# Attention and SoLU feed-forward on one core: earlier exp, mult and norm behind h, spreads of the last group after the next stage's loads, another bank for the last product, results stored by quarters

## The chip, the cores and the metric

The kernel runs on one core of a Trainium2 chip. The metric is the device time of one execution in microseconds (us). A core has a matmul engine (TensorE, PE; its weight loads are listed as PEld), a vector engine (VectorE, DVE), an engine for activation functions and copies (ScalarE, ACT), a general one (GpSimd, POOL), and a queue engine (SyncE, SP) from which most transfers are issued. Each engine works through its own list of instructions in order; an instruction that needs another engine's result waits for a semaphore, and everything behind it on its engine waits too. PE writes to banks of PSUM, from which DVE and ACT read.

## What is computed

Attention with normed queries and keys, then a feed-forward block whose activation is h times softmax(h), followed by a layer norm. All is float32, except the two weight matrices, which come as float64.

```python
q_n, k_n = rmsnorm(q, g_q), rmsnorm(k, g_k)       # (8, 12, 448, 64)
attn = softmax(scale * q_n @ k_n^T)
x = (attn @ v) laid out as (3584, 768)
h = x @ w_in                                      # (3584, 1024)
e = np.exp(h - h_max)
solu = h * (e / (sum(e) + 1e-09))
ln = (solu - mu) / np.sqrt(var + 1e-06) * g_ln    # over the 1024
out = ln @ w_out                                  # (3584, 768)
```

## The kernel before, in words

There are two programs in the kernel; the one that runs is `fast_path`. The other, `general_path`, stands behind a branch at the very end (L1666) that is not taken: every engine reads a flag and jumps over it.

`fast_path` has three stages, each paced by PE.

1. Attention, to about 331 us. It isn't touched.
2. The first product, h = x @ w_in, to 584 us, in 14 groups (`NG`) of 256 rows. Each group is two tiles of 128 rows: tile 2g and tile 2g+1. A group is computed by Winograd's form of a 2x2 block product, that is, with seven products in place of eight (`products`, L968). Each of P1 to P7 is one *unit* of three float32 matmuls, six instructions in the trace, 2.58 us.
3. The second product, ln @ w_out, in seven passes of 512 rows (`NS`), each with seven outer products (`outer_product`, L1177) which are again made of seven inner ones.

Units run in a list that `in_parts` writes out by hand. From the second group on the order of one group is P6, P5, P7, then P1 of the next group, P4, P2 of the next group, P3. P6 and P7 add to the bank (A) that P1 of the same group opened; P3 adds to the bank (B) of P5; P2 has bank C and P4 bank D. Between P1 and P6, and between P6 and P7, ACT copies the bank's content to SBUF (`part`, L989; the copies are called q1, u2 and u3), so P6 must not start before the copy q1 is made, nor P7 before the copy u2. The rest is added on DVE by `plus` (L998), which reads a bank and a copy and writes a half row of h, with its maximum.

When P4 is done, tile 2g+1 of h is complete (`done(1)`); when P3 is done, tile 2g is (`done(0)`). For each complete tile there follows a chain over four engines:

- `ff_max` (L1047, DVE): the negated maximum;
- `ff_exp` (L1053, ACT): exp of h, with its sum;
- `ff_mult` (L1057, DVE): h times the exp;
- `ff_moments` (L1065 to L1070 on DVE, then L1071 and L1073 on POOL): mean and variance, scale and shift;
- `ff_norm` (L1077, ACT): scale and shift applied;
- `ff_spread` (L1086, DVE, a transpose of 32x32 blocks into `ub`; then four transfers from SP, L1089, to `ud` in DRAM).

`later(x, f)` puts a step x units further back in the order: x = 1 means right behind the unit that is being written out, 2 behind the next one. The five numbers in `WAITS` are those of exp, mult, moments, norm and spread. The instructions stand on each engine in the order in which these calls come; nothing reorders them afterwards.

On the same queues lie, in groups 0 to 6, the conversions of w_out from float64 (`convert_w`): two passes on ACT (L535, L536), two joins on DVE (L541, L542), a product on ACT (L547), and its load from SP; and, later, sums of w_out's blocks on POOL (`combine_out`, L563), 44 in all. POOL also makes the four block sums of each next group's x (L962 to L966).

The third stage works on operands that are loaded back from `ud` (`load_u`, L1131). Six halves for the first pass are loaded during the second stage; six more loads (four of them of data that were loaded before, into other memory) stand at the start of the third stage, since they take memory that the first product's weights and x hold until then. `make` builds the operands: a12 (L1151), a22 (L1153), a11 (L1149) are copies on ACT, s1 to s4 are sums on DVE (s2 is L1157, s3 L1159, s4 L1161), and `inner_sums` (L1172 to L1175) runs on POOL. Its units are counted in *slots* of 0.65 us, four to a unit of `later`. In the third stage every inner product adds to banks A, B or C, and copies on ACT (L1206) or sums on DVE (L1208, L1226, L1238, L1246) empty them; inner P7 waits for the copy u2 of inner P6, inner P4 for the copy u3 of inner P7, as before. `store_y` (L1260) sends one quarter of a pass's result, 256 rows by 384 columns (384 KB), when its last piece is there.

In PSUM the first product's banks A and C come from a pool of three buffers with the tag "t", B and D from one of two with the tag "o"; the banks of the third stage lie where these were.

Of the kernel before, what the change touches and what calls it, by code (L numbers as in the profile page):

```python
# [366 lines left out]
def fast_path(  # L367
# [24 lines left out]
    nc = tc.nc  # L392
    B, H, S, D = q.shape
    DM, DFF = moe_w_in.shape
    P = 128
# [6 lines left out]
    HO = DM // 2  # L402
    NT = B * S // P
    NG = NT // 2
# [563 lines left out]
    def products(g, done):  # L968


        k = {}
        n = DFF // 2

        def mul(bank, a, i, begin=True):
            a11, a12, a21, a22 = gs[g, "A"]
            sm = gs[g, "s"]
            a = {"a11": a11, "a12": a12, "s3": a21, "a22": a22, "s1": sm[:, 0], "s2": sm[:, 1], "s4": sm[:, 2]}[a]
            if begin:
                tag = "t" if bank in "AC" else "o"
                k[bank] = ps_t.tile([P, 512], FP32, tag=tag, name=bank, bufs=3 if tag == "t" else 2)[:, 0:n]  # L980
            for c in range(HD):
                nc.tensor.matmul(  # L982
                    k[bank], a[:, c], w_in[i][:, c],
                    start=begin and c == 0, stop=c == HD - 1, skip_group_check=not begin,
                )

        def part(name, bank):
            k[name] = sums_in.tile([P, 512], FP32, tag="part", name=name, bufs=4)[:, 0:n]
            nc.scalar.copy(k[name], k[bank])  # L989

        def plus(row, col, bank, x):
            t = 2 * g + row
            d = mt.setdefault(t, {})
            out = half_of(t, col)
            top = small.tile([P, 1], FP32, tag="top", name="top")
            nc.vector.tensor_tensor_reduce(  # L998
                out, k[bank], k[x], 1.0, d.get("top", -3.4e38), OP.add, OP.max, top
            )  # L1000
            d["top"] = top

        def p1():
            mul("A", "a11", 0)
            part("q1", "A")

        def p2():
            mul("C", "a12", 1)
            plus(0, 0, "C", "q1")

        def p6():
            mul("A", "s2", 5, False)
            part("u2", "A")

        def p5():
            mul("B", "s1", 3)

        def p7():
            mul("A", "s3", 4, False)
            part("u3", "A")  # L1020
            plus(1, 1, "B", "u3")

        def p4():
            mul("D", "a22", 6)
            plus(1, 0, "D", "u3")
            done(1)

        def p3():
            mul("B", "s4", 2, False)
            plus(0, 1, "B", "u2")  # L1030
            done(0)

        return {1: p1, 2: p2, 3: p3, 4: p4, 5: p5, 6: p6, 7: p7}

    def half_of(t, i):
        d = mt.setdefault(t, {})
        if "h" not in d:
            d["h"] = big.tile([P, DFF], FP32, tag="h", name="h", bufs=3)
        return d["h"][:, i * DFF // 2 : (i + 1) * DFF // 2]
# [4 lines left out]
    def ff_max(t):  # L1044
        d = mt[t]
        d["nmax"] = small.tile([P, 1], FP32, tag="hmax", name="hmax")
        nc.vector.tensor_scalar(d["nmax"], d["top"], -1.0, None, OP.mult)  # L1047

    def ff_exp(t):
        d = mt[t]  # L1050
        d["u"] = big.tile([P, DFF], FP32, tag="u", name="u", bufs=3)
        d["s"] = small.tile([P, 1], FP32, tag="hsum", name="hsum")
        nc.scalar.activation(d["u"], d["h"], AF.Exp, bias=d["nmax"], accum_out=d["s"])  # L1053
# [40 lines left out]
    def in_parts():  # L1094
        def done(g, i):
            t = 2 * g + i
            ff_max(t)
            for x, f in zip(WAITS, (ff_exp, ff_mult, ff_moments, ff_norm, ff_spread)):
                later(x, lambda f=f: f(t))

        p = [products(g, lambda i, g=g: done(g, i)) for g in range(NG)]
        parts = [p[0][1], p[0][2]]
        for g in range(NG):
            turn = [p[g][6], p[g][5], p[g][7], p[g][4], p[g][3]]
            x = len(parts)
            if g + 1 < NG:
                turn[3:] = [p[g + 1][1], p[g][4], p[g + 1][2], p[g][3]]
            parts += turn
            if g + 1 < NG:
                follow(parts, x, lambda g=g: sizes(g + 1))  # L1110
                follow(parts, x + 1, lambda g=g: block_sums(g + 1, 0))
                follow(parts, x + 2, lambda g=g: block_sums(g + 1, 1))
            if g + 2 < NG:
                follow(parts, x + 4, lambda g=g: load_x(g + 2))
        return parts

    WAITS = (1, 2, 3, 5, 7)
    ORDER = ("P1", "P5", "P6", "P2", "P7", "P3", "P4")
    STEP = 7
    PLACES = (0, 4, 8, 10, 12, 16, 20)  # L1120
    NS = NT // 4
    KC = HF // 2
    N2 = HO // 2
    HALVES = {"P1": ("a11", 0), "P2": ("a12", 1), "P6": ("s2", 5), "P5": ("s1", 3), "P7": ("s3", 4), "P3": ("s4", 2), "P4": ("a22", 6)}
    last = {}
    us = {}
# [50 lines left out]
    def outer_product(n, name, q):  # L1177


        operand_name, area = HALVES[name]  # L1180
        k = {}

        def mul(bank, a, i, begin):
            x = us[n, operand_name]
            sm = us.get((n, operand_name, "sums"))
            a = {
                "a11": x[:, 0, 0:KC], "a12": x[:, 0, KC:], "a22": x[:, 1, KC:],
                "s1": sm and sm[:, 0], "s2": sm and sm[:, 1], "s3": sm and sm[:, 2], "s4": sm and sm[:, 3],
            }[a]
            if begin:  # L1190
                tag = f"{bank}{q % 2}" + (str(q // 2 % 2) if bank == "A" else "")
                k[bank] = last["ps"].tile([P, 512], FP32, tag=tag, name=bank)[:, 0:N2]
            for c in range(KC):
                nc.tensor.matmul(  # L1194
                    k[bank], a[:, c].rearrange("p a i -> p (a i)"), w_out[:, area, i, c],
                    start=begin and c == 0, stop=c == KC - 1, skip_group_check=not begin,
                )

        def quarter(x, t, i):
            return x[:, t, i * N2 : (i + 1) * N2]  # L1200

        def plus(out, bank, t, i):

            x = {"P6": "Q1", "P2": "Q1", "P7": "U2", "P4": "U3", "P3": "V"}.get(name)
            if x is None:
                nc.scalar.copy(out, k[bank])  # L1206
            else:
                nc.vector.tensor_tensor(out, k[bank], quarter(us[n, x], t, i), OP.add)  # L1208

        def temp(x):  # L1210
            k[x] = last["u"].tile([P, N2], FP32, tag=x, name=x, bufs=3)
            return k[x]

        def result(t, i):
            return quarter(us[n, name], t, i)

        def p1():
            mul("A", "a11", 0, True)
            plus(temp("q1"), "A", 0, 0)

        def p2():
            mul("C", "a12", 1, True)
            us[n, name] = out_tile(name)
            if name in ("P1", "P6", "P7"):
                us[n, {"P1": "Q1", "P6": "U2", "P7": "U3"}[name]] = us[n, name]
            nc.vector.tensor_tensor(result(0, 0), k["C"], k["q1"], OP.add)  # L1226

        def p6():
            mul("A", "s2", 5, False)
            plus(temp("u2"), "A", 0, 1)  # L1230

        def p5():
            mul("B", "s1", 3, True)

        def p7():
            mul("A", "s3", 4, False)
            plus(temp("u3"), "A", 1, 1)
            nc.vector.tensor_tensor(result(1, 1), k["B"], k["u3"], OP.add)  # L1238

        def p4():  # L1240
            mul("A", "a22", 6, False)
            plus(result(1, 0), "A", 1, 0)

        def p3():
            mul("B", "s4", 2, False)
            nc.vector.tensor_tensor(result(0, 1), k["B"], k["u2"], OP.add)  # L1246
            if name in ("P2", "P3", "P4"):
                store_y(n, us[n, name], *{"P2": (0, 0), "P3": (0, 1), "P4": (1, 0)}[name])

        return [p1, p2, p6, p5, p7, p4, p3]  # L1250

    def out_tile(name):
        tag = "huhuhubb"[len(turns) % 8]
        turns.append(tag)
        x = big.tile([P, DFF], FP32, tag=tag, name=name, bufs=2 if tag == "b" else 3)
        return x[:, 0 : 2 * HO].rearrange("p (t n) -> p t n", t=2)

    def store_y(n, x, k, i):
        r = (4 * n + 2 * k) * P
        nc.sync.dma_start(  # L1260
            out[r : r + 2 * P, i * HO : (i + 1) * HO].rearrange("(t p) n -> p t n", p=P), x
        )
# [9 lines left out]
    def follow(p, i, f):  # L1272
        g = p[i]

        def both():
            g()
            later(1, f)

        p[i] = both
# [7 lines left out]
    def later(units, f):  # L1287
        todo.append((now + 4 * units, f))
# [49 lines left out]
    with tc.manual_schedule():  # L1338
# [233 lines left out]
        for n in range(NS):  # L1572
            base = period * n
            for i, name in enumerate(ORDER):
# [4 lines left out]
                x = HALVES[name][0]  # L1579
# [118 lines left out]
```

## Time and profile before

| what | us |
|---|---|
| median of three runs | 827.21 (824.08, 829.25, 827.21) |
| the profiled execution | 824.41 |
| its span, from first to last instruction | 822.2 |
| first product on PE, from first to last unit | 331.7 to 584.4 |
| first instruction of the last stage on PE | 585.23 |
| last DVE result / last store issued | 816.05 / 816.43 |

The span is the time between the first and the last instruction of the profiled execution; 2.2 us of its time lie around it. The granted clock of PE is 1.00 in nearly all of the span (0.997 in the mean). The page's groups of instructions and the trace in order of time are what the steps below are read from; in a line of the trace in order of time the columns are the start, the length, the engine, the line of the source, the operation and its tiles with their shapes, and in brackets the idle time before it and who ended it. A line for a stretch lists for PE, PEld, DVE, ACT and POOL the busy time and the number of instructions, then the clock, the share of the transfer engines and the rate.

Some durations, minimum, median and maximum in us over the first product: mult L1057 1.18, 1.22, 1.65; join L541 0.52, 0.56, 1.29; exp L1053 1.15 and its read-out 0.19; norm L1077 1.24; copy L989 0.57; POOL's L1071 0.55, 0.93, 1.48 and L1073 0.26, 0.27, 1.36.

### The profile page before, as it was taken

What the parts mean: (1) busy time and instruction counts of PE and PEld (TensorE: products, weight loads), DVE (VectorE), ACT (ScalarE), POOL (GpSimd) and SP (SyncE); (2) the same over time, 40 slices, a digit from 0 to 9 for tenths busy, and PEclk for the clock granted to TensorE, in tenths of its full rate; (3) what the DMA queues carried; (4) which work ended last, traced back from release to release, by engine and by line L of the source; (5) the groups of instructions that cost most, each with busy time, mean ns of one, the idle gap of its engine ahead of it and who ended that gap; (6) DMA issues with size and microseconds to landing.
All of it is one profiled execution on the core that took longest, in us unless ns stands there. A gap on an engine that the chain in (4) does not pass through costs nothing.

```text
span 822.2 us, 14988 instructions
## 1 busy us (share of the span) xinstructions
PE 800.5 (97%) x5030; PEld 468.7 (57%) x5030; DVE 618.1 (75%) x1217; ACT 474.6 (58%) x785; POOL 468.7 (57%) x635
## 2 busy tenths in 40 slices
PE   8989999999999999999999999999799999999996
PEld 4333444433334443444444444444499999999996
DVE  6867888887788888377878766677886866866945
ACT  6667778776777767366667644444424464464420
POOL 1334545555555647333356467777387777877861
PEclk9999999999999999999999999999999999999999
DMA  7678777777777663335665335552448466376312
GB/s 132 142 134 200 145 183 177 176 153 171 154 176 180 126 156 117 89 102 125 189 169 150 91 98 133 136 140 70 140 142 269 130 207 231 128 241 200 128 59 82
DMA packets 271938, 122.74 MB, mean 149 GB/s; under 512 B 190444, under 2 KB 257004, under 8 KB 271852
## 3 DMA queue, kind: packets, MB, share of 16 engines
q1 hardware_dynamic: 256668, 111.79, 52.9%
q10 hardware_dynamic: 15184, 9.90, 4.5%
q8 instruction: 42, 0.69, 0.4%
q14 instruction: 44, 0.36, 0.1%
HBM read 84.94 MB, written 36.70 MB: 148 GB/s over the span
## 4 chain that ended last, share of the span: by engine, by line
PE 84%; SPq 2%; DVE 2%; issue 2%; POOL 1%; DMA 1%; ACT 1%; POOLq 0%; ACTq 0%; DVEq 0%
PE A L1194 15%; PE A L982 13%; PE o L865 10%; PE s L812 10%; PE B L982 8%; PE B L1194 8%; PE D L982 4%; PE C L982 4%; PE sm L884 4%; PE C L1194 4%; SPq L634 2%; PE s L825 2%; PE o L854 2%; POOL ss L674 1%; DMA ur<-ud 1%
## 5 line engine op out<-in xcount | busy, mean ns | idle before, releaser
L802 ACT ACTIVATE E<-s 128x896 f32<-128x896 f32 x168 | 139.0, 935 | 14.9 <-PE s L812 14.6
L812 PE MATMUL s<-qkT 64*64 64x448 f32 x1152 | 121.3, 548 | 1.5 <-ACT E L802 0.9
L865 PE MATMUL o<-E,v 128*64 128x448 f32 x576 | 113.5, 543 | 0.0
L674 POOL COPY ss<-part 32x56 f32<-32x56 f32 x88 | 42.1, 478 | 97.9 <-DVE part L664 95.2
L713 POOL TENSOR_TENSOR qkn<-qk,ny 128x896 f32<-128x896 f32 x46 | 77.1, 1697 | 28.2 <-DMA qk<-in_k_dram 12.0
L1071 POOL TENSOR_TENSOR he<-he,mhalf 128x1 f32<-128x1 f32 x28 | 28.1, 1005 | 106.7 <-DVE he L1070 106.2
L812 PEld LDWEIGHTS s<-qkT 64*64 64x64 f32 x1152 | 47.5, 163 | 61.1 <-ACT E L802 31.3
L865 PEld LDWEIGHTS o<-E,v 128*64 128x64 f32 x576 | 39.2, 137 | 72.7 <-issue 66.4
L1194 PE MATMUL B<-w_out,sums 128*128 128x192 f32 x392 | 80.5, 328 | 0.0
L1194 PE MATMUL A<-w_out,sums 128*128 128x192 f32 x392 | 80.0, 327 | 0.4 <-DVE u L1208 0.4
L982 PE MATMUL B<-w_in,xsum 128*128 128x512 f32 x168 | 76.7, 592 | 0.0
L982 PE MATMUL A<-w_in,xg 128*128 128x512 f32 x168 | 74.7, 593 | 0.0
L1053 ACT ACTIVATE u<-h,hmax 128x1024 f32<-128x1024 f32 x28 | 32.2, 1148 | 65.2 <-DVE hmax L1047 65.2
L1194 PEld LDWEIGHTS B<-w_out,sums 128*128 128x128 f32 x392 | 67.0, 191 | 0.1
L1194 PEld LDWEIGHTS A<-w_out,sums 128*128 128x128 f32 x392 | 66.2, 190 | 0.9 <-POOL sums L1175 0.6
L664 DVE TENSOR_REDUCE part<-sq 128x28 f32<-128x896 f32 x46 | 48.7, 1080 | 8.8 <-ACT sq L656 6.7
L982 PEld LDWEIGHTS B<-w_in,xsum 128*128 128x128 f32 x168 | 31.9, 190 | 40.2 <-issue 38.3
L982 PEld LDWEIGHTS A<-w_in,xg 128*128 128x128 f32 x168 | 31.8, 190 | 40.2 <-issue 39.1
L723 DVE STREAM_TRANSPOSE qkT<-qkn 128x896 f32<-128x896 f32 x46 | 48.9, 1093 | 6.6 <-POOL qkn L713 6.6
L839 DVE TENSOR_TENSOR es<-E 128x896 f32<-128x896 f32 x48 | 53.3, 1112 | 0.5 <-ACT E L802 0.5
L656 ACT ACTIVATE sq<-qk 128x896 f32<-128x896 f32 x46 | 43.6, 985 | 8.7 <-DMA qk<-in_k_dram 6.7
L1194 PE MATMUL A<-w_out,s 128*128 128x192 f32 x224 | 45.6, 326 | 0.0
(151 smaller groups left out, 1625.3 us busy)
## 6 DMA issues: line engine op xcount, KB each, us to landing
ur<-ud SPq DMA_DIRECT2D x60, 256.0 KB, 4.7
ud<-ub SPq DMA_DIRECT2D x112, 128.0 KB, 2.3
xd<-xo SPq DMA_DIRECT2D x24, 448.0 KB, 3.7
qk<-in_q_dram SPq DMA_DIRECT2D x184, 56.0 KB, 2.5
qk<-in_k_dram SPq DMA_DIRECT2D x184, 56.0 KB, 2.4
v<-in_v_dram SPq DMA_DIRECT2D x24, 384.0 KB, 4.4
out_dram<-P SPq DMA_DIRECT2D x21, 384.0 KB, 3.8
raw<-in_moe_w_in_dram SPq DMA_DIRECT2D x12, 512.0 KB, 5.2
```

The costliest lines, as they stand in the source:

```text
L656: nc.scalar.activation(d["sq"], d["qk"].rearrange("p s b d -> p (s b) d"), AF.Square)
L664: nc.vector.tensor_reduce(norms[m]["part"][:, i], st[n]["sq"], AX, OP.add)
L674: e.tensor_copy(ss[g * 32 : g * 32 + 32], part[o * 32 : o * 32 + 32])
L713: e.tensor_tensor(d["qkn"], d["qk"].rearrange("p s b d -> p (s b) d"), y.rearrange("p b -> p b ()").to_broadcast([P, 2 * NB, 32]), OP.mult,)
L723: nc.vector.transpose(d["qkT"].rearrange("p s t -> p (s t)"), d["qkn"].rearrange("p b d -> p (b d)"))
L802: nc.scalar.activation(d["E", kc], s[:, :, 0:S], AF.Exp)
L812: nc.tensor.matmul(s[c : c + D, h, 0:S], d["qkT"][hh, 1, keys], d["qkT"][hh, 0, :], start=True, stop=True,)
L839: nc.vector.tensor_tensor(d["es"], d["E", 0], d["E", 1], OP.add)
L865: nc.tensor.matmul(d["o"][h * D : (h + 1) * D, :], quads[n // 2]["v"][:, n % 2 * 2 + h, kc], d["E", kc][:, h], start=False, stop=(kc == NJ ...
L884: nc.tensor.matmul(sm[g : g + 32, :], ones[:, w], e[:, h, t * S // 2 : (t + 1) * S // 2], start=(x == 0), stop=(x == len(terms) - 1),)
L982: nc.tensor.matmul(k[bank], a[:, c], w_in[i][:, c], start=begin and c == 0, stop=c == HD - 1, skip_group_check=not begin,)
L1194: nc.tensor.matmul(k[bank], a[:, c].rearrange("p a i -> p (a i)"), w_out[:, area, i, c], start=begin and c == 0, stop=c == KC - 1, skip_gr ...
```

## The change

Five edits. (1) The exp of a tile is written out at once when the tile is complete, and mult, moments, norm and spread follow 1, 2, 3 and 5 units behind instead of 2, 3, 5 and 7. Since 1 means right behind the same unit, mult now stands directly behind the tile's last plus on DVE. (2) For the two tiles of the last group the distances are 1, 2, 4 and 8. (3) In the last group P5 and P3 use a bank of the pool "t" and not of "o". (4) In the last pass of the third stage the outer products P3 and P4 are stored in four pieces each, of 128 rows by 192 columns (96 KB), as each piece is made, and not in one transfer of 384 KB at the end: eight transfers in place of two. (5) `store_y` is called for the same three outer products as before in all other cases.

```diff
-                tag = "t" if bank in "AC" else "o"
+                tag = "t" if bank in "AC" or bank == "B" and g == NG - 1 else "o"
...
             ff_max(t)
-            for x, f in zip(WAITS, (ff_exp, ff_mult, ff_moments, ff_norm, ff_spread)):
+            ff_exp(t)
+            for x, f in zip(LAST_WAITS if g == NG - 1 else WAITS, (ff_mult, ff_moments, ff_norm, ff_spread)):
                 later(x, lambda f=f: f(t))
...
-    WAITS = (1, 2, 3, 5, 7)
+    WAITS = (1, 2, 3, 5)
+    LAST_WAITS = (1, 2, 4, 8)
...
+        block = {"P2": (0, 0), "P3": (0, 1), "P4": (1, 0)}.get(name)
+        by_quarter = n == NS - 1 and name in ("P3", "P4")
+
+        def stored(t, i):
+            if by_quarter:
+                store_quarter(n, us[n, name], *block, t, i)
...
             nc.vector.tensor_tensor(result(0, 0), k["C"], k["q1"], OP.add)
+            stored(0, 0)
...
             nc.vector.tensor_tensor(result(1, 1), k["B"], k["u3"], OP.add)
+            stored(1, 1)
...
             plus(result(1, 0), "A", 1, 0)
+            stored(1, 0)
...
             nc.vector.tensor_tensor(result(0, 1), k["B"], k["u2"], OP.add)
-            if name in ("P2", "P3", "P4"):
-                store_y(n, us[n, name], *{"P2": (0, 0), "P3": (0, 1), "P4": (1, 0)}[name])
+            stored(0, 1)
+            if block and not by_quarter:
+                store_y(n, us[n, name], *block)
...
+    def store_quarter(n, x, k, i, t, half):
+        r = (4 * n + 2 * k + t) * P
+        c = i * HO + half * N2
+        nc.sync.dma_start(out[r : r + P, c : c + N2], x[:, t, half * N2 : (half + 1) * N2])
```

In the order of instructions this moves the following. On ACT the exp of tile 2g is now followed by the norm of tile 2g+1 and then by the copy u2 of the next group; before, u2 came ahead of that norm. On DVE mult and moments of tile 2g+1 now both stand ahead of the plus that completes tile 2g; before, mult stood ahead of it and moments behind it. On SP the four transfers of tile 24 now stand ahead of the third stage's first six loads (before: only those of tile 25), and the last group's transfers behind two more loads of the second pass.

## The prediction

> **What bounds the kernel now.** I read the page first (engine shares, the chain), then TensorE's waits, then three stages, then one group of the first feed-forward product on each engine.
>
> ```profile
> PE 800.5 (97%) x5030; PEld 468.7 (57%) x5030; DVE 618.1 (75%) x1217; ACT 474.6 (58%) x785; POOL 468.7 (57%) x635
> PE 84%; SPq 2%; DVE 2%; issue 2%; POOL 1%; DMA 1%; ACT 1%; POOLq 0%; ACTq 0%; DVEq 0%
> ```
>
> TensorE (PE) is the bound. Its waits list only two that the change can touch:
>
> ```profile
> engine line waited for: us in total, times, longest us
> PE A L1194 <- ACT u L1206: 4.5, 1, 4.5
> PE A L1194 <- DVE top L998: 0.9, 1, 0.9
> ```
>
> The stages of x@w_in, of the transition, and of the end (busy us per engine):
>
> ```profile
> 331.70:584.40 252.70, 252.68 (x592) 111.53 (x588) 179.26 (x384) 137.16 (x224) 139.96 (x160) 1.00 0.46 121
> 584.40:600.00 15.60, 10.24 (x51) 9.95 (x52) 12.64 (x28) 7.68 (x15) 6.57 (x9) 0.89 0.85 254
> 816.40:822.20 5.80, 0.00 (x0) 0.00 (x0) 0.01 (x1) 0.00 (x0) 0.00 (x0) 0.90 0.35 120
> ```
>
> In the first, PE idles 0.02 of 252.70 us: a shorter chain behind h can gain nothing there, only lose. In the second it idles 5.4; the end is 5.8. So some 11 us at most can be had. Now DVE, ACT and PE around one boundary of groups, in time:
>
> ```profile
> 390.52 1.18 DVE L1057 TENSOR_TENSOR u<-h,u 128x1024 f32<-128x1024 f32 x1
> 391.62 0.55 DVE L541 SCALAR_TENSOR_TENSOR tmp<-raw,tmp 128x384 uint32<-128x384 uint32 x1
> 392.68 0.74 DVE L998 CUSTOM_DVE_ANT_0 h<-B,u,top 128x512 f32<-128x512 f32 x1
> 393.54 1.28 DVE L1065 BATCH_NORM_STATS2 bs<-u 128x6 f32<-128x512 f32 x2
> 395.50 1.22 DVE L1057 TENSOR_TENSOR u<-h,u 128x1024 f32<-128x1024 f32 x1
> ```
>
> ```profile
> 393.65 1.15 ACT L1053 ACTIVATE u<-h,hmax 128x1024 f32<-128x1024 f32 x1 [0.24 <-DVE hmax L1047]
> 394.80 0.56 ACT L989 COPY u<-A 128x512 f32<-128x512 f32 x1
> ```
>
> ```profile
> 391.00 2.74 PE L982 MATMUL A<-w_in,xsum 128*128 128x512 f32 x6
> 393.58 2.74 PE L982 MATMUL B<-w_in,xsum 128*128 128x512 f32 x6
> 396.15 4.03 PE L982 MATMUL A<-w_in,xg 128*128 128x512 f32 x9
> ```
>
> P6 fills bank A from 391.00, P5 bank B, and P7 at 396.15 adds to A again: it may start only when ACT has copied u2 out of A. That copy ended at 395.36, 0.8 us in time. It stands right behind one exp.
>
> **The chain in order.** In the changed kernel's instruction order, ACT has between that exp (tile 2g) and u2 now also the norm of tile 2g+1 (L1077), and DVE has mult and moments of tile 2g+1 ahead of the plus (L998) that this exp waits for. I walk one group, zero being when plus takes D (350.00 in the first group; P7 starts 10.27 later, at 360.27).
> - exp starts 0.99 after (350.99) and is read out 1.24 later: 2.23. mult now waits for it, nothing hides that; DVE's next comes 1.13 on (585.28 to 586.41): 3.38.
> - plus of C, 0.62 (388.74 to 389.36): 4.00. Moments, 1.96 (393.54 to 395.50): 5.96.
> - plus of B to exp 0.97 (392.68 to 393.65): 6.93. Then 1.15 to ACT's next (393.65 to 394.80): 8.08. The norm's scale is ready 3.99 after the moments began (573.28 to 577.27): 7.99, just in time.
> - norm, 1.15 to ACT's next (593.86 to 595.01): u2 at 9.23; 0.56 and 0.06 to its reader (595.81 to 595.87): 9.85. Slack 0.42.
>
> Conversions of w_out share these queues in groups 0 to 6. The order puts a pair of joins (L541, L542: 1.06, 391.62 to 392.68) between moments and plus, and a product (L547, 0.6) between norm and u2, twice (u2 of groups 3 and 6): 9.85 + 1.06 + 0.6 - 10.27 = 1.24 late; another pair and a spread stand ahead of plus D there, so DVE also begins late, by 0 to 0.8; I take 0.4, so 1.64 each. Twice (groups 1 and 4) the pair L535, L536 (1.09, 397.08 to 398.17) stands between norm and u2: 0.67 late, once plus the 0.6 us that L535 waited for its raw DMA. Sum: 2 x 1.64 + 0.67 + 1.27 = 5.2. The nine other groups keep 0.42; POOL's shift (L1073) took 0.26 to 1.36 us, so some lose a little: 0.1 each, 0.9. **In-stage +6.1.** Bounds: 0 if the fast rows hold everywhere, and 11.6 if the nine lose 0.4 each (3.6) and both groups with joins meet slow ones (1.25 and 1.29 instead of 0.56 each, as at 365.28: 1.4 more, 2.8). A gain is excluded by the 0.02 us.
>
> On the joins: L542 took 1.23 at 343.80 beside POOL's L963, and 0.56 at 351.60 with POOL idle. The Trainium skill, page "SBUF — State Buffer", section "Who interferes with whom", says that a DVE instruction with two SBUF inputs contends with a GpSimd instruction that reads SBUF; mult (1.22, once 1.65) only partly agrees. By that rule the sum is up to 2.8 higher; I keep the fast row, the median.
>
> **Transition.** The last plus now reads a bank that A of the last stage doesn't take: the 0.85 us wait at 585.23 goes. What is late next: DVE takes the spread of tile 24 at 582.81 (in place of tile 25's), mult of tile 27 at 584.14 (its exp, 582.88 + 1.24, ends then), plus of B at 585.27 (was 584.41); exp of tile 26 starts at 586.24 (was 585.46) and the q1 copy behind it holds the second A product: the 0.85 is given back. On SP tile 24's four ud stores stand where tile 25's stood (584.09 to 585.92), so the six loads start at 586.03 as before. Then ACT, before:
>
> ```profile
> 593.34 0.62 ACT L1151 COPY a<-ur 128x512 f32<-128x512 f32 x1 [4.89 <-DMA ur<-ud]
> 593.86 1.24 ACT L1077 ACTIVATE u<-u,shift,he 128x1024 f32<-128x1024 f32 x1
> 595.01 0.60 ACT L1151 COPY a<-ur 128x512 f32<-128x512 f32 x1
> 595.51 0.30 ACT L1206 COPY u<-A 128x192 f32<-128x192 f32 x1
> ```
>
> The u3 copy at 595.51 ends the 4.5 us wait. Now tile 26's norm stands between the halves of a12 (before: tile 27's, ready by then). Tile 26: moments of 27 at 586.13 (plus + 0.86), mult at 588.09 (+1.96), two s2 from 589.22 (+1.13), P1's plus at 590.42 (+1.20), moments at 590.69 (+0.27), norm at 594.68 (+3.99), second a12 at 595.83 (+1.15), u3 at 596.33 (+0.50), PE at 596.69 (+0.36), against 595.87: **+0.8**. Fewer stores beside the loads (512 KB go earlier) may land a12 sooner, but the norm is then last. Bounds: L1071 took 0.55 to 1.48 us and 1.46 is in my row: -0.1 up to +0.8; a shift of 1.36 makes it +1.9. The spreads of the last group, 8 units out, pass two loads of n=1 on SP; PE idles 0.06 of 205 us from 600 to 805, so nothing.
>
> **End.** The last store is issued at 816.43 now too. SP's branch (L1666) at 816.9 is followed by its next instruction at 820.2, DVE's from 817.0 to 820.5; ACT, branching at 806.1, went on at 808.7. The store's landing (3.8 us by the page's median, about 820.2) and the branch end together. Eight quarter issues (about 0.4 each) are spread over 10 us; four in the last 1.7 us just fit, the last two 0.65 apart. A quarter lands sooner (128 KB ud: 2.3), the branch not surely: gain 0 if it stays 3.4, 0.8 if it becomes ACT's 2.6. **-0.4.**
>
> Page "DMA: Bandwidth & Descriptors", section "Anatomy of one DMA — SWDGE (gpsimd) path", gives about 2.0 us fixed per DMA, most of it the write receipt, which speaks against splitting stores. By it the last quarter lands at about 818.5, an estimate, and the branch alone decides.
>
> **Sum.** The profiled run is 824.41 (span 822.2 and 2.2 around), 2.80 under the median of three, 827.21. 824.41 + 6.1 + 0.8 - 0.4 = 830.9; with 2.8, **833.7** (+0.8%).
>
> **Rivals.** (a) Slower than 1%: one mechanism, DVE at its slow rows beside POOL at the boundary; it decides once a group's lag passes 0.42 us. In-stage 11.6, transition +0.8, end -0.4: 839. For: POOL is busy 140 of 252.7 us; against: medians are the fast rows. (b) The copies stay in time, because DVE's and ACT's queues run ahead of my walk (u2 had 0.8 spare here): in-stage 0, transition -0.85 as the bank's wait is saved whole, end -0.8: 825.6. Against: mult's wait for its exp and the norm ahead of u2 are in the order. (c) The losses come but half as large (raw DMAs early, DVE not late): 2.6, +0.5, -0.4: 830.
>
> **Numbers.** Forecast with (c), 829 to 835.4: 0.54; (a), above 835.5: 0.30; (b), 822 to 829: 0.16, of which 0.03 under 819. About 1% (8.3 us) is what a measurement of this kernel can tell from no change: faster 0.03, same 0.67, slower 0.30. The range 825.5 to 839.0 takes in (b)'s and (a)'s points.
>
> **What would show it.** PE waits "A L982 <- ACT u L989" of 0.7 to 1.6 us in four groups, none elsewhere; the first A of the last stage without wait, but three waits after it (q1, u2, u3), the last ending 12.3 us after the stage began; a last store of 96 KB landing well before the branch returns. PE without a gap before 584 would make me wrong, and then (b) holds.

## The result, and the profile after

The changed kernel took 836.2 us (median of four runs, 834.3 to 836.4) where the kernel before took 825.6 in the runs beside it: ratio 1.0122, 95% interval 1.0073 to 1.0172. The profiled execution took 834.3, its span is 832.2. Against the profiled execution of before (span 822.2) the 10.0 us more are made up so, read from the starts of TensorE's products: attention +0.5, x@w_in from its first to its last product 252.1 to 263.4 (**+11.3**), from there to the last product of the last stage 231.9 to 230.3 (**-1.6**), the end -0.1.

TensorE's waits, from the list of who waited for whom of the changed kernel (us in total, times, longest; L1196 and L1208 are L1194 and L1206 of before):

```profile
PE A L982 <- ACT u L989: 5.1, 4, 3.1
...
PE A L982 <- issue: 2.8, 3, 1.7
...
PE A L1196 <- ACT u L1208: 2.5, 2, 2.2
...
PE A L1196 <- ACT q L1208: 1.3, 1, 1.3
```

The wait for the bank (DVE top L998) is gone, the single wait of 4.5 has become three, and the first line is new: P7 waits for the copy u2. Some of the waits for u2 stand under "issue". From the starts of the products the waits ahead of P7 are 0.82 (group 1), 1.88 (3), 1.29 (4), 3.29 (6), and 0.56, 0.60 and 0.62 (9, 10, 13). The stages by windows (length, busy us of PE, PEld, DVE, ACT, POOL, granted clock, DMA share, GB/s):

```profile
332.15:595.95 263.80, 255.88 (x592) 111.51 (x589) 187.39 (x386) 135.68 (x224) 130.80 (x160) 0.99 0.44 118
595.95:611.55 15.60, 11.79 (x60) 10.73 (x59) 11.64 (x29) 8.52 (x17) 9.20 (x12) 0.89 0.77 236
```

In the first row PE idles 7.9 us instead of 0.02, and is busy 3.2 us longer with the same products; 1.4 of that is a stretch of half clock, shown below, and most of the rest lies around the restarts behind the waits. The longest wait, group 6, in time (start, length, engine, line, operation):

```profile
439.93 1.24 ACT L1077 ACTIVATE u<-u,shift,he 128x1024 f32<-128x1024 f32 x1 [0.97 <-POOL shift L1073]
...
442.17 0.57 ACT L989 COPY u<-A 128x512 f32<-128x512 f32 x1
...
442.77 0.69 DVE L998 CUSTOM_DVE_ANT_0 h<-B,u 128x512 f32<-128x512 f32 x1 [2.57 <-ACT u L989]
...
443.38 0.87 DVE L541 SCALAR_TENSOR_TENSOR tmp<-raw,tmp 128x384 uint32<-128x384 uint32 x1
443.81 1.31 POOL L966 TENSOR_TENSOR xsum<-xg,xsum 128x384 f32<-128x384 f32 x1
444.29 1.24 DVE L542 SCALAR_TENSOR_TENSOR tmp<-raw,tmp 128x384 uint32<-128x384 uint32 x1
...
446.61 0.70 DVE L998 CUSTOM_DVE_ANT_0 h<-D,u,top 128x512 f32<-128x512 f32 x1
...
452.34 2.74 PE L982 MATMUL B<-w_in,xsum 128*128 128x512 f32 x6
...
455.87 1.23 ACT L1077 ACTIVATE u<-u,shift,he 128x1024 f32<-128x1024 f32 x1
...
457.00 0.60 ACT L547 ACTIVATE w_out<-tmp,gcol 128x384 f32<-128x384 f32 x1
457.50 0.56 ACT L989 COPY u<-A 128x512 f32<-128x512 f32 x1
...
458.21 1.19 PE L982 MATMUL A<-w_in,xg 128*128 128x512 f32 x1 [3.13 <-ACT u L989]
```

P5's six products start 0.43 apart from 452.34, so P7 was due at 454.92; it started at 458.21. Ahead of u2 stand the norm and the product L547, as walked. But already the plus of D, the walk's zero, started at 446.61, where 10.27 before 454.92 is 444.65: DVE was 1.96 late. Ahead of it stand two joins that took 0.87 and 1.24 beside POOL's L965 and L966, and ahead of these a plus of B that had waited 2.57 for the copy u3 (442.17); that copy stood on ACT behind a norm (439.93) which had waited 0.97 for its shift. And what came behind the wait:

```profile
454.20:457.60 3.40, 0.88 (x3) 0.05 (x1) 2.02 (x5) 2.88 (x5) 0.76 (x1) 1.00 0.63 188
457.60:461.00 3.40, 2.79 (x4) 1.27 (x5) 2.80 (x8) 3.34 (x8) 1.51 (x3) 0.50 0.00 0
```

TensorE sat idle 2.5 of the first 3.4 us, and in the next 3.4 its granted clock is 0.50: the three products behind P7's first started 0.56, 0.42 and 0.42 later than they should.

### The profile page after: what moved, and what is told of

Its sections match the earlier page's. It is cut to its first block, busy times and chain, and to the rows that moved or that the text cites. A ratio compares the mean times of both kernels' runs of the same rounds, so it can differ in the third digit from the quotient of the medians.

```text
span 832.2 us, 14975 instructions
## 1 busy us (share of the span) xinstructions
PE 804.5 (97%) x5030; PEld 468.6 (56%) x5030; DVE 623.5 (75%) x1217; ACT 472.7 (57%) x785; POOL 460.6 (55%) x635
## 4 chain that ended last, share of the span: by engine, by line
PE 70%; SPq 6%; DVE 5%; DMA 3%; issue 3%; ACT 3%; POOL 1%; ACTq 0%; DVEq 0%; POOLq 0%
PE A L1196 15%; PE A L982 12%; PE B L1196 7%; PE o L865 7%; PE s L812 7%; PE B L982 6%; SPq L634 5%; PE D L982 4%; PE C L1196 4%; PE C L982 3%; PE sm L884 3%; DMA v<-in_v_dram 2%; PE s L825 1%; PE o L854 1%; DVE h L998 1%
## 5 line engine op out<-in xcount | busy, mean ns | idle before, releaser
L1071 POOL TENSOR_TENSOR he<-he,mhalf 128x1 f32<-128x1 f32 x28 | 18.1, 648 | 124.5 <-DVE he L1070 124.5
L1196 PE MATMUL A<-w_out,sums 128*128 128x192 f32 x392 | 80.8, 329 | 3.9 <-ACT u L1208 2.2
L982 PE MATMUL A<-w_in,xg 128*128 128x512 f32 x168 | 76.6, 605 | 7.9 <-ACT u L989 5.1
L1196 PE MATMUL B<-w_out,sums 128*128 128x192 f32 x392 | 79.8, 326 | 0.0
L1196 PEld LDWEIGHTS A<-w_out,sums 128*128 128x128 f32 x392 | 66.7, 191 | 4.8 <-issue 4.0
L1196 PEld LDWEIGHTS B<-w_out,sums 128*128 128x128 f32 x392 | 66.2, 190 | 0.1
L1057 DVE TENSOR_TENSOR u<-h,u 128x1024 f32<-128x1024 f32 x28 | 40.5, 1446 | 27.9 <-ACT u L1053 27.5
L563 POOL TENSOR_TENSOR w_out<-w_out 128x384 f32<-128x384 f32 x44 | 48.7, 1111 | 1.0
```

The source lines that it names most:

```text
L563: nc.gpsimd.tensor_tensor(o, p, q, OP.subtract)
L982: nc.tensor.matmul(k[bank], a[:, c], w_in[i][:, c], start=begin and c == 0, stop=c == HD - 1, skip_group_check=not begin,)
L1196: nc.tensor.matmul(k[bank], a[:, c].rearrange("p a i -> p (a i)"), w_out[:, area, i, c], start=begin and c == 0, stop=c == KC - 1, skip_gr ...
```

## The experiments

All of them together; "in" is x@w_in from first to last product, "out" from there to the last product of the last stage, both in us of the profiled execution; the ratio is to the kernel before on the same chip.

| kernel | in | out | ratio | 95% interval |
|---|---|---|---|---|
| before | 252.1 | 231.9 | | |
| changed | 263.4 | 230.3 | 1.0122 | 1.0073 to 1.0172 |
| old_chain | 252.1 | 233.3 | 1.0007 | 0.9989 to 1.0025 |
| norm_later | 254.7 | 230.5 | 1.0019 | 1.0000 to 1.0038 |
| moments_later | 257.4 | 230.6 | 1.0065 | 1.0042 to 1.0088 |
| norm_spread_later | 261.8 | 231.6 | 1.0139 | 1.0102 to 1.0175 |
| moments_spread_later | 259.0 | 234.6 | 1.0067 | 1.0041 to 1.0093 |
| stores_later | 253.2 | 232.4 | 0.9987 | 0.9967 to 1.0008 |
| conv_shift | 265.8 | 232.2 | 1.0138 | 1.0090 to 1.0185 |
| bank_only | 252.1 | 232.9 | 0.9990 | 0.9976 to 1.0004 |
| keep_busy | 252.4 | 233.4 | 1.0013 | 0.9999 to 1.0027 |
| best | 252.6 | 228.4 | 0.9956 | 0.9934 to 0.9978 |
| best2 | 252.1 | 226.6 | 0.9938 | 0.9914 to 0.9962 |
| best3 | 252.4 | 226.9 | 0.9922 | 0.9899 to 0.9945 |

### Is the loss the chain's? (old_chain)

```diff
-            ff_exp(t)
+            if g == NG - 1:
+                ff_exp(t)
+            else:
+                later(1, lambda: ff_exp(t))
...
-    WAITS = (1, 2, 3, 5)
+    WAITS = (2, 3, 5, 7)
```

> The changed kernel with the old chain behind h (exp, mult, moments, norm, spread in the old order) for groups 0 to 12; the last group's order, the bank of the last product and the stores by quarters stay changed. Theory (the whole loss lies in the chain of groups 0 to 12, on ACT and DVE ahead of the copy u2): the in-stage falls from 263.4 back to 252.1 +-0.5 us, PE shows no wait A L982 <- ACT u L989, and the time is that of before or up to 2 us less (the transition was 1.6 us shorter in the changed kernel's profile): 823.5 to 826 where before is 825.6. Rival (part of the loss lies in the other three edits, or the clock's half-speed stretch comes whatever the chain): 828 or more, or a half-speed stretch inside the in-stage without a gap.

The in-stage is that of before to the hundredth (252.11), with no wait in it; the time is 826.7 against 826.0, ratio 1.0007. So the whole loss is the chain's, in groups 0 to 12, and the other three edits bring nothing that can be measured. The shorter transition did not come along: with group 12's spreads at 7 again a transpose (1.24 us at 588.48) stood ahead of the moments of tile 26 on DVE, its norm waited 2.28 for the shift, and the copy u3 came late (a wait of 3.0 us); and 3.4 us of half clock lay over full work behind it.

### The norm ahead of u2 (norm_later)

```diff
-    WAITS = (1, 2, 3, 5)
+    WAITS = (1, 2, 4, 5)
```

> The changed kernel with the norm of groups 0 to 12 one part later (waits 1, 2, 4, 5 instead of 1, 2, 3, 5): on ACT the norm of tile 2g+1 stands behind the copy u2, DVE's order is the changed one, mult and moments ahead of the plus of B. Theory A (the norm ahead of u2 is the largest term, 1.15 of each group's lag; what DVE adds is the rest): each wait for u2 shrinks by 1.15, so the groups with 0.82, 1.88, 1.29, 3.29 us keep 0, 0.7, 0.1 and 2.1, the three of 0.6 vanish, and no gap reaches 3 us, so the clock keeps full speed: in-stage 255.0 (+2.9), time 827 (825.5 to 829). Rival B (mult and moments on DVE ahead of the plus of B hold the copies; the norm only waits beside them): the waits keep at least two thirds of their size, in-stage 259 or more, time 831 or more.

The in-stage fell by 8.7 us to 254.65 (2.9 over before was expected, 2.5 came), the time to 828.1. Of the four waits 0, 0.36, 1.39 and 0.64 are left, the three small ones and the half clock are gone. Theory A holds: one number out of place on ACT made three quarters of the loss. Group 6 lost more than the 1.15 of its norm, 2.65 (0.64 where 2.1 was expected): the same number had put a norm ahead of the copy u3 as well, and with that norm behind the copy the plus of D of group 6 is 0.45 late and not 1.96. But group 4 did not shrink (1.29 before, 0.1 expected). ACT's rows and SP's queue there (SPq are DMA issues):

```profile
415.27 0.66 ACT L535 ACTIVATE tmp<-raw,seven 128x384 f32<-128x384 uint32 x1 [1.46 <-DMA raw<-in_moe_w_out_dram]
...
416.39 0.57 ACT L989 COPY u<-A 128x512 f32<-128x512 f32 x1
```

```profile
401.18 5.97 SPq L1089 DMA_DIRECT2D ud<-ub  x8
407.26 8.07 SPq L515 DMA_DIRECT2D raw<-in_moe_w_out_dram  x8
```

Behind the norm stood another late thing: L535 waits 1.46 us for its raw load of w_out, and u2 stands behind L535. SP issued the eight ud stores of two tiles first, and then took 8 us over eight raw loads, because they wait for landings of the x-loads (SP's waits there: 4.6 us for xg<-xd, in two parts). All DMAs of the program take turns on eight semaphores (in this trace 100 or 101 DMAs on each), each waiting for the one eight places before it: the raw load issued at 413.17 waited for an x-load that landed at 413.15. An order of SP that puts a raw load eight places behind a long x-load makes it wait.

### Which part of the spread? (norm_spread_later, stores_later)

```diff
-    WAITS = (1, 2, 4, 5)
+    WAITS = (1, 2, 4, 7)
```

> As the kernel with the later norm (waits 1, 2, 4, 5), and with the spread back at 7: the ud stores of groups 0 to 12 stand on SP where they stood in the kernel before. Theory (what is left of the wait in group 4, 1.39 us, is ACT's L535 waiting 1.46 us for its raw load of w_out, which SP issued late because the ud stores now stand ahead of it and the loads share semaphores with the long xg loads): L535's wait falls to the 0.61 us of before, the wait for u2 in group 4 falls to 0.5 or less, the other two stay (0.36, 0.64): in-stage 252.9 to 253.7, time 826 to 827 where before is 826.0. Rival (the raw load is late because its buffer comes free late, when the joins on DVE read it, whatever the stores do): group 4 keeps 1.0 or more, in-stage 254.3 or more.

A miss: L535 no longer waits, as the theory had it, but the in-stage is 261.8, group 4 has still 0.94, groups 3 and 6 rose to 1.76 and 2.54, groups 5 and 9 to 12, which had no wait in norm_later, lost 0.24 to 0.67 each, and the half clock is back. The spread is a transpose on DVE and four stores, and the transpose (1.24) had moved with them to a place ahead of the moments and of the plus of B. exp's longest wait for hmax went from 4.8 to 6.0. So only the stores were moved:

```diff
-    WAITS = (1, 2, 4, 5)
+    WAITS = (1, 2, 4, 5, 7)
...
-            for x, f in zip(..., (ff_mult, ff_moments, ff_norm, ff_spread)):
+            for x, f in zip(..., (ff_mult, ff_moments, ff_norm, ff_turn, ff_store)):
```

> As the kernel with the later norm (waits 1, 2, 4, 5; in-stage 254.65 us), and the spread of groups 0 to 12 split: its transpose stays at 5, where it was, its four ud stores go to 7. Nothing moves on DVE, PE or POOL; only SP's order changes. (In the kernel with the whole spread at 7 the transpose, 1.24 us, had moved ahead of the moments and the plus of B, and the in-stage became 261.8: that run could not tell the stores apart.) Theory (the 1.39 us left in group 4 is L535's raw load, issued late on SP behind the ud stores and behind the landing of an xg load): L535 waits 0.7 or less in place of 1.46, group 4's wait is 0.7 or less, the others stay as they were (0.36, 0.64): in-stage 252.9 to 254.0, time 0.5 to 1.5 us under that kernel's. Rival (the raw load comes late for its buffer or for the busy DMA engines): 1.1 or more stay in group 4, in-stage 254.3 or more.

Group 4's wait and L535's are gone entirely, 0.37 and 0.64 stay in groups 3 and 6, in-stage 253.19. SP's queue of that kernel at the same place:

```profile
402.84 1.72 SPq L515 DMA_DIRECT2D raw<-in_moe_w_out_dram  x4
404.66 6.81 SPq L1092 DMA_DIRECT2D ud<-ub  x4
411.58 1.77 SPq L515 DMA_DIRECT2D raw<-in_moe_w_out_dram  x4
```

Now the stores wait for the x-load and nobody waits for them. With the norm one part and the stores two parts later than in the change, and mult, moments and transposes as early, the time is that of before (0.9987): the shorter chain is then free, and brings nothing.

### DVE's share (moments_later, moments_spread_later)

```diff
-    WAITS = (1, 2, 3, 5)
+    WAITS = (1, 3, 4, 5)
```

> As the kernel with the later norm, and with the moments one part later too (waits 1, 3, 4, 5): DVE takes the plus of B ahead of the moments of tile 2g+1; only exp and mult stand earlier than in the kernel before. Theory (mult alone costs 1.15 of DVE ahead of the plus of B, u2 has some 4 us to spare): in-stage 252.1 to 252.7, time 823.5 to 825.5 (the shorter transition kept). Rival (any reordering that puts mult, which waits for exp, ahead of the plus of C makes DVE late beside the conversions of w_out): waits for u2 stay in the groups 3 and 6, in-stage 254 or more, time 827 or more.

A miss, with the in-stage and the time on the rival's side: 257.4, with 0.98, 2.64 and 1.13 us in groups 3, 4 and 6. With the moments later the norms wait for their shift (12 times, 18.4 us in all, between 340 and 480 us; no such wait in norm_later), and in group 4 L535 waited 2.68 us for its raw load, 1.2 more than in norm_later, as group 4's wait did. The next run put the spread back as well (waits 1, 3, 4, 7).

> As the kernel with the later moments (waits 1, 3, 4, 5), and with the spread back at 7. That kernel's in-stage was 257.4, with a wait of 2.64 us for u2 in group 4, behind an L535 that waited 2.68 us for its raw load. Theory (SP's order made that wait): group 4 falls to 0.6 or less and the 0.98 and 1.13 us in groups 3 and 6 to half or less, since their u2 stands behind the same late loads: in-stage 252.1 to 253.5, time 825.5 to 827. Rival (plus of B ahead of the moments makes the norm late, and the norm the copies behind it, whatever SP does): 1.5 us or more stay in group 4, in-stage 255 or more, time 828.5 or more.

In-stage 259.0, not 253: 1.61, 2.13 and 1.35 us are left, and half clock behind the second. L535 still waited 1.9 us for its load in group 4, so the stores' old place alone did not bring the load in time. The run moved the transpose too, as above, so neither theory is settled by it: of the 2.7 us that the later moments cost, 1.2 go with L535's load, and what made the rest stays open. The version with late moments and only the stores late was not tried.

### Do the conversions size the waits? (conv_shift)

```diff
-            follow(parts, 3 * (x - n_in) + 2, lambda x=x: convert_next(x))
+            follow(parts, 3 * (x - n_in) + 3, lambda x=x: convert_next(x))
```

(The combinations on POOL one part later with them.)

> The changed kernel with the conversion of w_out (and its combinations on POOL) one part later: in the instruction order the joins ahead of the plus of B and the product L547 ahead of u2 now fall in groups 1, 4 and 7, the pair L535, L536 in groups 2 and 5, and groups 3 and 6 are free of both. Theory (the size of a group's wait is what the conversions put in its queues): waits for u2 of 1.6 to 3.3 us in groups 1, 4 and 7, of 0.7 to 1.4 in 2 and 5, none over 0.7 in 3 and 6; in-stage 262 to 266; a half-speed stretch only behind a gap of 3 us or so. Rival (groups 3 and 6 are long for another reason, their x-loads or POOL's sums): 1.5 us or more stay in 3 and 6.

The waits moved as the order says: 1.43 (1.6 was the least expected), 2.07 and 3.30 us in groups 1, 4 and 7, 0.87 and 0.94 in 2 and 5, none in 3 and 0.26 in 6. Group 7 is the image of group 6: a norm that waited 0.96 ahead of the copy u3, joins of 0.87 and 1.23, a plus of D that is 1.97 late. Its clock, though, behaves otherwise, and not as expected:

```profile
415.80:419.20 3.40, 1.49 (x4) 0.46 (x3) 2.58 (x4) 3.40 (x6) 0.00 (x0) 1.00 0.41 125
419.20:422.60 3.40, 3.40 (x6) 1.31 (x5) 2.86 (x7) 3.31 (x7) 2.54 (x4) 0.50 0.17 39
473.80:477.20 3.40, 2.26 (x6) 0.71 (x4) 2.02 (x6) 1.49 (x3) 1.09 (x2) 1.00 0.07 19
477.20:480.60 3.40, 1.40 (x4) 0.71 (x5) 3.17 (x8) 3.37 (x6) 0.21 (x1) 1.00 0.02 5
```

The 2.07 us of group 4 brought half clock (second row), the 3.30 us of group 7 did not: they fell into two windows of 3.41 us (1.18 and 1.96 idle), the 2.07 into one (1.91 idle).

### The bank alone (bank_only)

```diff
-                tag = "t" if bank in "AC" else "o"
+                tag = "t" if bank in "AC" or bank == "B" and g == NG - 1 else "o"
```

> The kernel before with one edit: the last group's bank B comes from tag t. Theory (the 0.85 us wait for the bank goes and is given back at the copy u3 behind the loads, 4.5 us): last in-stage product to last out-stage product unchanged within 0.3 us, time equal to before within 0.3%. Rival 1 (the wait is saved whole): 0.85 us less, 0.1%. Rival 2 (the shift of 0.85 us moves the half-speed stretch of 3.4 us off full work, as in the changed kernel): 1.5 to 2.5 us less, 0.25%.

The 0.85 us for the bank went and came back as 0.88 at the copy q1; u3's wait stayed (4.7). 0.9990, within what can be told from no change: the theory holds for the waits. Out grew by 1.0 where 0.3 was the most expected, since the half clock lasted 6.8 us here instead of 3.4.

### Is it the idle time that halves the clock? (keep_busy)

```diff
+        def keep_busy():
+            x = last["ps"].tile([P, 512], FP32, tag="C0", name="busy")[:, 0:N2]
+            a = us[0, "a11"][:, 0, 0].rearrange("p a i -> p (a i)")
+            for i in range(24):
+                nc.tensor.matmul(x, a, w_out[:, 0, 0, 0], start=i == 0, stop=i == 23)
+
+        when(15, keep_busy)
```

> The kernel before with 24 products of 128x192 more, into a bank that nothing reads, placed on TensorE ahead of the fourth quarter of the last stage's first product, where it stood idle for 4.7 us (nothing is left out; 24 x 0.163 = 3.9 us of otherwise idle time). Theory (the 3.41 us of half clock that begin at 595.7 in the kernel before, over full work, are the answer to the idle time just ahead of them): the granted clock stays 1.0 there, the out-stage shortens by 1.67 us, the time by as much: 823 to 824 where before is 824.6, and no wait grows. Rival (the half clock comes whatever TensorE does at that place, or the added products delay the copy u3): the stretch of 0.5 is still there, time equal or up to 1 us more.

The stretch of half clock was gone (granted clock 1.00 throughout, 0.51 there before), so it does answer to the idle time. The time was not better: the rows count these products as 48, and they took 7.8 us, not 3.9, some 2.8 beyond the end of the copy u3, more than the 1.7 won.

### The transition without its waits (best, best2, best3)

On the kernel before, with its chain and stores:

```diff
+    LAST_WAITS = {
+        2 * NG - 3: (1, 2, 3, 5, 7, 9), 2 * NG - 1: (1, 3, 5, 7, 8, 8), 2 * NG - 2: (2, 4, 5, 7, 9, 9),
+    }
...
+            waits = LAST_WAITS.get(t, WAITS + WAITS[-1:])
-            for x, f in zip(WAITS, (ff_exp, ff_mult, ff_moments, ff_norm, ff_spread)):
+            for x, f in zip(waits, (ff_exp, ff_mult, ff_moments, ff_norm, ff_turn, ff_store)):
...
-        for h in range(2):
-            for t in (2, 3):
-                load_u(0, t, h)
-        for t in range(2):
-            load_u(0, t, 1)
+        for t, h in ((0, 1), (1, 1), (2, 0), (3, 0), (2, 1), (3, 1)):
+            load_u(0, t, h)
...
-        made(0, "s2", 0, 3)
-        made(0, "s3", 6, 8)
-        made(0, "a12", 10, 11)
-        made(0, "a22", 12, 14)
-        made(0, "s4", 17, 20)
+        made(0, "s2", 0, 2)
+        made(0, "a12", 13, 14)
+        made(0, "s3", 17, 19)
+        made(0, "a22", 21, 22)
+        made(0, "s4", 24, 26)
```

with the bank of bank_only, and the next quad's loads, a11 and s1 up to 7 slots later.

> The kernel before with its own chain behind h, the other bank for the last product, and the start of the last stage reordered: the stores of tile 25 go behind the six loads, a12's two loads come first, a12 is made after the copy u3, s3, a22, s4 and the next quad's loads later, exp of tile 26 behind the copy q1, the norms of the last group behind u3 (stores as before). Theory (the 4.7 us wait and the 0.85 for the bank are nothing but ACT's order and SP's): in-stage 252.1, no wait over 1 us in the first 20 us of the last stage, last in-stage product to last out-stage product 231.9 - 5.5 = 226.4, and with no such gap no half-speed stretch there either, 1.7 less: time 819 (817.5 to 821.5). Rival (the work put off makes operands late further on, in the second or third product of the last stage): waits of 3 us or more in all come back there, time 823 or more.

0.9956: 3.6 us faster, half of what was expected. The waits of the transition (in the kernel before for the bank and for u3, in the changed one for q1, u2 and u3) and the half clock are gone; 3.7 us of other waits came further on (0.36, 1.53, 0.65, 1.12), so half of the rival is true too. best2 moves tile 26's moments and norm to 6 and 8 (its spread stays at 9, unlike what is said below) and the next quad's sums some slots on:

> The kernel with the reordered start of the last stage (252.6 in-stage, 3.7 us of waits in the last stage's first 26 us, span 821.6), with moments, norm and spread of tile 26 another part later (so POOL takes a12's sums ahead of tile 26's pow, and DVE the plus of the second product ahead of its moments) and s1, s2, s3, s4 of the next quad 1 to 11 slots later. Theory (what was left there was this one queue of moments and next operands): the waits of 1.53, 0.65 and 1.12 fall to 1.2 in sum, last in-stage product to last out-stage product 226.5 (228.4 before), time 1.5 to 2.5 us under that kernel's, ratio to before 0.993 to 0.994. Rival (DVE has more work than time in these 25 us, whatever the order): the waits come back elsewhere, 2.5 us or more in sum, ratio 0.9955 or more.

Out 226.6, as expected, with 0.35, 1.53 and 0.29 us of waits left, 2.2 in sum where 1.2 was expected; 0.9938. Its first 15.6 us of the last stage, where before PE worked 10.2 and the changed kernel 11.8 us:

```profile
579.65:595.25 15.60, 14.04 (x83) 13.21 (x82) 14.76 (x33) 9.20 (x20) 10.80 (x15) 1.00 0.49 134
```

> The last kernel with one number changed: the moments of tile 26 another part later (slot 23 in place of 19), so that on DVE the plus of the second product's last quarter (L1257) no longer stands behind them. Theory (the 1.53 us that was left at that quarter's bank B is DVE's 1.96 us of moments ahead of its plus): that wait falls to 0.5 or less, first to last out-stage product 225.1 to 225.6 (226.2 before), time 1 us less, ratio to before 0.992 to 0.994. Rival (DVE is full there, and the moments push the next plus instead): 1 us or more comes back within the next 20 us, ratio 0.994 as before.

The wait of 1.53 went, one of 1.56 and one of 0.5 came some 4 us later, at another plus of DVE: the rival holds, the row above shows why (DVE 14.8 of 15.6 us). best2 and best3 (0.9938 and 0.9922) can't be told apart; both beat the kernel before and the changed one.

## Why the prediction was right, and where it was not

The time, 836.2, lies in the range, but outside the forecast's own band (829 to 835.4): it is 0.7 into that of rival (a), which had a chance of 0.30. Against the kernel before it is +10.6 us where +6.5 was forecast. In the profile the in-stage cost 5.2 more than its sum and the transition 2.4 less, and the kernel before has a median 1.6 under the 827.2 that the sum was added to; that 836.2 came so near to 833.7 is in part luck. By its steps:

- **The walk of one group** was right to 0.1 us: from the plus of D to P7 it gave 9.85 + 1.06 + 0.6 = 11.51 for the groups with joins; the rows show 11.55 in group 3 and 11.60 in group 6. The groups it named were groups that waited. Two readings in it are a little off: 2.23 + 1.13 is 3.36, not 3.38, and P7's first product in the first group starts at 360.10; 360.27 is where the chain's view lets it begin. So the slack was 0.25 and not 0.42, and 0.17 of each lateness below, which are measured with the 10.27, is that.
- **"DVE also begins late, by 0 to 0.8; I take 0.4"** failed in group 6. The plus of D was 0.60 late in group 3 and 1.96 in group 6: 1.88 and 3.29 instead of 1.64 each. In group 6 the two joins ahead of it took 1.0 us more than the 0.56 each that was taken for joins. But joins as slow stood there in the kernel before, and the plus of D was late there too, by the same measure 1.20 (P7 started at 450.31), more than the 0.8 at most:

```profile
438.91 1.24 DVE L542 SCALAR_TENSOR_TENSOR tmp<-raw,tmp 128x384 uint32<-128x384 uint32 x1
...
441.24 0.70 DVE L998 CUSTOM_DVE_ANT_0 h<-D,u,top 128x512 f32<-128x512 f32 x1
```

The other 0.8 is the change's: the copy u3 ahead of these joins came that much later, behind the norm that waited for its shift. The walk asked what the norm does to the copy u2, and not what it does to u3. norm_later, where the norm stands behind the copy u3, tells the two apart:

```profile
441.08 1.24 DVE L542 SCALAR_TENSOR_TENSOR tmp<-raw,tmp 128x384 uint32<-128x384 uint32 x1
...
443.41 0.70 DVE L998 CUSTOM_DVE_ANT_0 h<-D,u,top 128x512 f32<-128x512 f32 x1
```

The joins are as slow (1.16 and 1.24), and the plus of D is 0.45 late (P7 was due at 453.23). So slow joins alone don't make the longest wait; with the late copy u3 they do. conv_shift moved the joins and the pair L535, L536 ahead of u3 together, so it shows only that the wait follows the conversions.

- **Groups 1 and 4**: 0.82 and 1.29 for 0.67 and 1.27. The first is off by the 0.17. That the second was met is luck in part: L535 waited 0.23 for its load there and not the 0.6 taken.
- **The nine others**: 1.8 in three of them (groups 9, 10 and 13), twice the 0.9, and for another reason. No norm waits for POOL's shift in these three; mult, which the walk took at 1.22, ran 1.94, 2.02 and 2.00 beside POOL's sums of w_out, in group 10:

```profile
523.44 4.01 POOL L563 TENSOR_TENSOR w_out<-w_out 128x384 f32<-128x384 f32 x3
...
524.57 2.02 DVE L1057 TENSOR_TENSOR u<-h,u 128x1024 f32<-128x1024 f32 x1 [1.31 <-ACT u L1053]
```

norm_later has no wait in any of the three.

- **A term that the sum lacked**: half clock after a long wait, 1.40 us in the in-stage. The last 1.0 us are the 0.08 that follows each restart and smaller gaps. 7.28 + 1.78 + 1.40 + 1.0 - 0.2 (gaps that before had too) = 11.3.
- **Transition +0.8**: the product that waits for u3 started 12.12 us after the in-stage's last product, where before had 12.09: +0.03. The mechanism (bank's wait given back, three waits, tile 26's norm between a12's halves) is in the rows; the pow took 0.86 and not the 1.46 taken, and the plus of B came 0.27 sooner, both inside the bounds named. That the stage ended 1.6 us earlier is the clock again: before, 3.41 us of half clock lay over full work behind the wait; in the changed kernel they began at 604.4, under the waits (3.41 / 2 = 1.7).
- **End -0.4**: -0.1. SP's branch took 2.70 us in place of 3.32, but some 0.5 us came back among the last steps of GpSimd. Nor did the quarters land well before the branch returned, as the prediction had it among its signs: the one issued at 825.91 landed at 829.56, after 3.65 us where 2.3 was taken and the estimate by the page's figure, which its section gives for GpSimd's own transfers, had 2.1; and SP went on at 829.69 (the last one's landing is not in the trace). The eight traces with quarters end 6.3 to 7.5 us after their last product, the six without 6.5 to 6.8: quarters bring nothing here.
- **Other signs**: four waits came, of 0.82 to 3.29 for 0.7 to 1.6, but three more beside them, where none was to be; the last wait of the transition ended 11.7 us after the stage began, not 12.3.
- **Rivals**: (a) named the in-stage's size (11.6), and DVE at slow rows beside POOL is in the trace, in the joins and in mult; but its make-up was another: its nine groups lost half of what it took, and the late copy u3 and the half clock are not in it. (b) fell with the first line of the waits, (c) with an in-stage of +11.3 for its 2.6.

## What to carry to other kernels

Where the bound engine has no idle time, an earlier step can only get in the way: look at what it is put ahead of on each queue, and move with care the one that stands ahead of the copy that frees a bank (here a norm of 1.23 us, three quarters of the loss). A step that also issues DMAs moves them too, and they can hold back loads that share their semaphores; split it, and move the parts apart. A walk along the queues is good to 0.1 us from a known start, so spend the effort on how late that start is: read it in the trace for every group that differs (1.20 stood there for group 6), and ask what the same move does to the copy that sets it.

## What the runs showed of the hardware

**The clock answers to the idle share of a fixed window.** In each trace the granted clock changes at multiples of 3.413 us (in the changed kernel at 457.617 and 604.390, 43 times that apart), and a window at half clock follows a window in which TensorE was idle long enough. Over the two last stages of all fourteen traces, worked out from the rows of PE: every one of the 11 windows with 2.18 us or more idle was followed by half clock, none of those with 1.75 or less that ran at full clock was; of five with 1.91 to 2.00, two were (1.91 and 1.97, but not 1.92, 1.96 and 2.00). So the two waits of conv_shift, of which the larger part of 3.30 us passed (1.96) and that of 2.07 did not (1.91), lie where the idle time does not decide alone, and what does is not shown. Of the 18 windows at half clock in these stages five were followed by another, with 0.58 to 1.06 us idle; the other 13 had 0.73 or less. The Trainium skill, "TensorE: Matmul & The Clock Gate", section "What's actually happening", describes such a free-running window and half clock after at least one idle window of about 3.4 us; the window agrees, but here some 2.2 us idle in it were enough. That idle time is the cause, and does not merely go with it, is shown by keep_busy for one place.

**A join beside POOL took 1.24 us instead of 0.56**, in the same queue and at the same size. In all fourteen traces the 274 joins with none of POOL's 128x384 sums beside them took 0.52 to 0.60; of the 167 that had such sums beside them for 60% of their time or more the median is 1.23 (0.52 to 1.40). mult took up to 2.02 in the changed kernel (in group 10), though not every mult beside such a sum was slow. The Trainium skill, "SBUF — State Buffer", section "Who interferes with whom", expects it of a DVE instruction with two SBUF inputs beside a GpSimd one that reads SBUF; the joins agree (0.87 and 1.24 beside L965 and L966 in group 6). The sum by that rule had been 2.8 us for two groups; of that the joins ahead of the plus of D brought 1.0 in group 6 and 0.3 in group 3 (0.88 and 0.56).
